# A two-stage attention kernel on one core: dummy matmuls on a tile of ones ahead of TensorE's work, and an instruction order laid out again

## The chip, the core and the metric

The kernel runs on one core of a Trainium2 chip. The core has five engines that run side by side: PE (TensorE, matmuls), DVE (VectorE), ACT (ScalarE), POOL (GpSimd) and SP (SyncE, which here only issues DMAs). The metric is the device time of one execution in microseconds; lower is better.

## The reference

```python
scores = np.matmul(q, k.transpose(0, 1, 3, 2)) / 8          # 8 batches, 8 heads, 576 rows, 64 columns
scores = np.where((rel >= 0) & (rel < 64), scores, -1e9)    # stage 1: a window of 64 keys
attn = softmax(scores)
x = (attn @ v).transpose(0, 2, 1, 3).reshape(8, 576, 512)
logits = x @ w_gate                                         # stage 2: 4 experts, the best 2 of each row
for e in range(4):
    q, k, v = x @ wq[e], x @ wk[e], x @ wv[e]               # 512 -> 64
    a = softmax(causal(q @ k.T / 8))
    out += weight[e] * (a @ v @ wo[e])                      # 64 -> 512
```

Stage 1 is attention in a window of 64 keys for 64 pairs of batch and head; stage 2 is causal attention of four experts per batch, weighted by a gate.

## The kernel before

**Work.** Stage 1 goes by units of eight blocks of 64 queries: scores (`s`), softmax on ACT, DVE and POOL, transposes (`t`) and the product with v (`a`). Two heads lie side by side on the 128 partitions as a "pair"; 32 pairs are loaded from HBM, each as q, k and v, into rings of three buffers. So the load of v for pair p waits until the last `a` block that reads pair p-3 is done, and one for q or k until the last such `s` block is. Stage 2 goes by batch and by pair of experts, 16 of these "expert pairs": projections (`K`, `k`, `Q`, `q`, `V`, `W`), scores (`1` to `4`, `0`), softmax, transposes, product with v (`A` and `B`) and the output projection (`O`, `o`). For 14 of the 16 expert pairs the transposes are done without PE: DVE transposes 32x32 blocks into the buffer `st2` and 16 DMAs move them within SBUF into `pt2` (rows `pt<-st`, `pt2<-st2`), 8 of 32x928 and 8 of 32x640 elements. I call these 16 DMAs a **set**; there are 14 sets, in the order of the expert pairs. `A` and `B` of an expert pair read the whole of its set, and its set may overwrite `pt2` only when `A` and `B` of the pair before are done. The last two expert pairs use PE transposes (`T`, `U`).

**Order.** Nothing is scheduled by hand line by line. Every instruction is recorded by a `Plan`; the string `ORDER` gives PE's blocks letter by letter, and the other engines' instructions are put in order by a small model of the core (`Plan.order`) that plays the program with costs of its own, one due time for each instruction, and the table `EARLY` of corrections to due times. Of a DMA the model takes a transfer time and `op["land"]`, the time until its data may be read. The model only lays the order out: on the chip each engine takes its instructions in that order and waits on semaphores. SP is one queue: a DMA whose buffer is not free holds up all that stand behind it. Its DMAs also share eight completion semaphores in turn, so that a DMA waits for the landing of the one eight places ahead. Every instruction is issued through line 381 (382 after the change).

**Start.** Inputs come as one stream of loads: three pairs at first and a fourth in `st2`, then the weights, then pair 4 and on. The letter `z` is a dummy block: two matmuls of `ident` with itself that nothing reads (`warm`). Six of these lie among the first blocks.

Of the kernel before, what the change touches and what calls it, by code (L numbers as in the profile page):

```python
# [34 lines left out]
    "sszzsztstazazstKKVtssQaatQsVtastkqaatzss1tV2aaVt0s3s4WVqtVVkqQ132aV4s0tKQKtksaAa"  # L35
    "B132qta40kQtKsssAaBOO1324tqOV0VOtkKaaBAsstV132a0VQtkqaABass41tVWVOVOKOtqssa3240t"
    "OKOQkaBAatVk13240qtQQsssBaAaVtVOV13240VtOQsstOOqKqaBaAatKk13240qtkssaBAWVOVtOOQs"
    "s13240VKVtOOkaaAB1324tKQk0qssaaABtOO13s24tOO0KQktqBaAa13240VtVqVVaaABOWKOOQk1324"
    "0KOVqOQVBAVkKV13240QkqBAT1TOT23T4U0TUOTUOUTUOTAUBUooUoUoUoABOOOOO"
)  # L40
EARLY = {
# [52 lines left out]
}  # L94
HOLD = 13000.0
TAIL = 2
SHORT = 0
WARM = 6
TPE = 99
BPOS = 0.05  # L100
SJOIN = 1
PARTS = ((0, 5), (5, 9))
# [294 lines left out]
def window_attention_moe_attention(ctx: ExitStack, tc: tile.TileContext, qT, kT, vW,  # L397
# [710 lines left out]
    for t, f, args in todo:  # L1108
        f(*args)
    with tc.manual_schedule():  # L1110
        nc.issue()
# [54 lines left out]
```

## Time and profile before

| what | value |
|---|---|
| median of three timed runs | 424.93 us (424.13 to 425.73) |
| the profiled execution, device time | 423.19 us |
| its span, first to last instruction | 421.5 us (1.69 us lie outside it) |
| mean granted clock of PE | 0.996 |
| PE busy | 404.1 us of 421.5 |
| loaded from HBM, written to it | 39.85 MB, 9.44 MB |

The page of the profile gives busy times by engine; the trace behind it tells what each engine waited for, which DMA landed when, and which clock PE was granted (1.00 is 2.4 GHz, 0.50 is 1.2 GHz). A float32 matmul stands in the trace as two MATMUL records, one with rounded operands (float32r) as one.

### The profile page before, as it was taken

To read this page: it belongs to the slowest core of one execution; us is meant where nothing else is said; L and a number is where in the kernel's file an instruction comes from. 1 tells how busy PE (TensorE), PEld (TensorE's weight loads), DVE (VectorE), ACT (ScalarE), POOL (GpSimd) and SP (SyncE) were. 2 spreads that over 40 slices of the span, in tenths; PEclk is the share of its full clock that TensorE was granted. 3 is DMA by queue.
4 is the path that set the end of the run, shared out by engine and by line. 5 is a ranking of instruction groups with operands and counts; after the bars stand their busy time and mean duration, and the time that the engine had idled before them with its cause. 6 is when DMAs were issued, how large, how long until landed. Compare 5 with 4: busy or idle time off the path is not lost. (4 is left out here: it accounts for less than half of the span.)

```text
span 421.5 us, 13748 instructions
## 1 busy us (share of the span) xinstructions
PE 404.1 (96%) x5168; PEld 364.4 (86%) x5168; DVE 310.3 (74%) x997; ACT 269.6 (64%) x854; POOL 276.2 (66%) x473
## 2 busy tenths in 40 slices
PE   5799999999999999999699999999899999999995
PEld 4688989999899989899598998998889999998874
DVE  4899997879876876768677878679696756456722
ACT  3676685767685858566558566585567754727932
POOL 4778777697879687695687949567759553505310
PEclk9999999999999999999899999999999999999999
DMA  7979661467876572478776366369645623642113
GB/s 241 337 260 318 187 212 59 108 167 222 283 203 188 136 252 90 122 183 299 199 223 182 136 180 201 103 157 302 173 155 139 167 56 104 166 101 54 51 51 124
DMA packets 33361, 72.66 MB, mean 172 GB/s; under 512 B 6160, under 2 KB 10256, under 8 KB 33296
## 3 DMA queue, kind: packets, MB, share of 16 engines
q1 hardware_dynamic: 32640, 71.14, 56.6%
q8 instruction: 41, 0.67, 0.6%
q10 hardware_dynamic: 656, 0.66, 0.5%
q14 instruction: 24, 0.20, 0.1%
HBM read 39.85 MB, written 9.44 MB: 117 GB/s over the span
## 5 line engine op out<-in xcount | busy, mean ns | idle before, releaser
L381 POOL TENSOR_SCALAR_AFFINE_SELECT pt<-ft 64x512 f32<-64x512 f32 x126 | 83.6, 663 | 38.2 <-ACT ft L381 29.0
L381 POOL TENSOR_TENSOR sm<-sm,st 128x512 f32<-128x512 f32 x72 | 76.5, 1068 | 34.3 <-DVE st L381 24.2
L381 POOL TENSOR_SCALAR p<-p,r,g 128x320 f32<-128x320 f32 (+4 forms) x135 | 83.5, 633 | 11.9 <-DVE r L381 10.5
L381 PE MATMUL o<-pt,v 128*64 128x64 f32 (+2 forms) x1776 | 82.5, 250 | 6.3 <-DMA pt<-st 3.2
L381 ACT ACTIVATE p<-p,r 128x192 f32<-128x192 f32 (+4 forms) x135 | 77.9, 579 | 15.8 <-DVE r L381 15.5
L381 PEld LDWEIGHTS o<-pt,v 128*64 128x64 f32 x1776 | 69.7, 139 | 20.2 <-issue 7.4
L381 DVE STREAM_TRANSPOSE st<-p 128x128 f32<-128x128 f32 (+5 forms) x126 | 63.5, 521 | 19.0 <-POOL p L381 9.9
L381 DVE CUSTOM_DVE_ANT_0 p<-s,causal 128x320 f32<-128x320 f32 (+2 forms) x120 | 52.7, 482 | 3.7 <-PE s L381 3.3
L381 DVE TENSOR_REDUCE st<-sm 128x8 f32<-128x512 f32 x72 | 47.9, 674 | 5.6 <-ACT sm L381 5.0
L381 PE MATMUL s<-k,q 64*64 64x128 f32 (+1 forms) x1116 | 37.0, 277 | 5.3 <-DMA q<-in_qT_dram 5.0
L381 PE MATMUL s<-kt,qt 64*128 64x256 f32 (+2 forms) x480 | 41.9, 317 | 0.0
L381 PEld LDWEIGHTS s<-kt,qt 64*128 64x128 f32 x480 | 35.1, 185 | 4.4 <-issue 1.8
L381 PEld LDWEIGHTS s<-k,q 64*64 64x64 f32 x1116 | 30.9, 139 | 9.2 <-DMA k<-in_kT_dram 4.5
L381 PE MATMUL kps<-xh,wkhi 128*128 128x256 f32 (+1 forms) x128 | 38.8, 303 | 0.0
L381 PE MATMUL qps<-xh,wqhi 128*128 128x320 f32 (+1 forms) x128 | 38.6, 302 | 0.0
L381 PE MATMUL v2ps<-wvhi,xh 128*128 128x260 f32 x128 | 37.8, 296 | 0.0
L381 PE MATMUL qps<-xl,wqhi 128*128 128x320 f32 (+1 forms) x128 | 37.7, 294 | 0.0
L381 PE MATMUL qps<-xh,wqlo 128*128 128x320 f32 (+1 forms) x128 | 37.6, 294 | 0.0
L381 PE MATMUL kps<-xl,wkhi 128*128 128x256 f32 (+1 forms) x128 | 37.6, 294 | 0.0
L381 PE MATMUL kps<-xh,wklo 128*128 128x256 f32 (+1 forms) x128 | 37.6, 294 | 0.0
L381 PE MATMUL v2ps<-wvhi,xl 128*128 128x260 f32 x128 | 36.3, 284 | 0.0
L381 PE MATMUL v2ps<-wvlo,xh 128*128 128x260 f32 x128 | 36.2, 283 | 0.0
(125 smaller groups left out, 928.9 us busy)
## 6 DMA issues: line engine op xcount, KB each, us to landing
v<-in_vW_dram SPq DMA_DIRECT2D x28, 576.0 KB, 5.4
pt<-st SPq DMA_DIRECT2D x112, 116.0 KB, 2.3
pt<-st SPq DMA_DIRECT2D x112, 80.0 KB, 2.1
out_dram<-out SPq DMA_DIRECT2D x32, 256.0 KB, 2.2
q<-in_qT_dram SPq DMA_DIRECT2D x28, 288.0 KB, 4.5
k<-in_kT_dram SPq DMA_DIRECT2D x28, 288.0 KB, 4.9
v<-in_vW_dram SPq DMA_DIRECT2D x3, 320.0 KB, 8.3
out_dram<-out SPq DMA_DIRECT2D x7, 128.0 KB, 2.4
```

Of the source, the lines that this page charges most:

```text
L381: call(*args, **kw)
```

## The change

Three things are changed. A tile `ones` is set on DVE, and three dummy blocks `y`, two 128x128x128 matmuls of it each, become PE's first work. In `Plan.add`, `land` grows from 1650 to 2750 ns for moves within SBUF and from 2300 to 3000 ns for loads. `ORDER` and `EARLY` are replaced by tables found for these numbers; `FIT` gets an entry for `y` (its cost is doubled in the model).

```diff
 ORDER = (
-    "sszzsztstazazstKKVtssQaatQsVtastkqaatzss1tV2aaVt0s3s4WVqtVVkqQ132aV4s0tKQKtksaAa"
...
+    "yyyszszzsztstzaazstKVtKssaaQtVsQtastkaqtass1tV2aa30tVss4WVktQqVKV1Va324s0tQqktKa"
...
 EARLY = {
-    0: 2100, 1: -1350, 2: 3350, 4: 5800, 5: 5300, 6: -8850, 7: 8050, 8: 72150, 9: 80300, 10: 5100,
...
+    3: -850, 4: 8900, 5: -7400, 6: -4000, 7: 13950, 8: 91150, 9: 75700, 10: 11400, 11: -4300, 12: 117550,
...
-            op["land"] = 1650 if len(inner) == 2 else 2300 if outs[0].space == bass.MemoryType.SB else 500
+            op["land"] = 2750 if len(inner) == 2 else 3000 if outs[0].space == bass.MemoryType.SB else 500
...
+    ones = const.tile([128, 128], F32, name="ones")
+    nc.vector.memset(ones, 1.0)
+    for k in range(3):
+        ps = psum.tile([128, 512], F32, tag="s", bufs=8, name=f"start_{k}")
+        with nc.block("y"):
+            for i in range(2):
+                nc.tensor.matmul(ps[:, 0:128], lhsT=ones, rhs=ones, start=True, stop=True)
```

Both ORDER strings hold the same number of every letter, 385 in all, and the new one three `y` more. What follows is what stands where in the built programs.

**PE, its first rows.** Before, the first block of scores stands first (`s1_0_0` and `s1_0_1` are its two banks, k0 and q0 the first pair, k1 and q1 the second):
```order
L381 MATMUL s1_0_0_108<-k0_76,q0_75 64x64 x2
L381 MATMUL s1_0_1_109<-k0_76,q0_75 64x128 x2
L381 MATMUL s1_0_0_108<-k0_76,q0_75 64x128 x2
L381 MATMUL s1_0_1_109<-k0_76,q0_75 64x128 x2
L381 MATMUL s1_0_0_108<-k1_78,q1_77 64x64 x2
L381 MATMUL s1_0_1_109<-k1_78,q1_77 64x128 x2
L381 MATMUL s1_0_0_108<-k1_78,q1_77 64x128 x2
L381 MATMUL s1_0_1_109<-k1_78,q1_77 64x128 x2
```
After:
```order
L382 MATMUL start_0_969<-ones_968 128x128 x2
L382 MATMUL start_1_970<-ones_968 128x128 x2
L382 MATMUL start_2_971<-ones_968 128x128 x2
L382 MATMUL s1_0_0_108<-k0_76,q0_75 64x64 x2
L382 MATMUL s1_0_1_109<-k0_76,q0_75 64x128 x2
L382 MATMUL s1_0_0_108<-k0_76,q0_75 64x128 x2
L382 MATMUL s1_0_1_109<-k0_76,q0_75 64x128 x2
L382 MATMUL s1_0_0_108<-k1_78,q1_77 64x64 x2
```
The three dummy blocks now precede the first scores; one `warm` block follows these (further down, not shown).

**SP, ahead of the sixth set.** v19 to v21, q22, k22, q23 and k23 are loads of stage 1's pairs, `out_1_2` and `out_1_3` stores of results, `pt2<-st2` the moves of the set. Before:
```order
L381 DMA v19_499<-in_vW_dram 128x1152
L381 DMA out_0_dram<-out_1_3_480 128x512
L381 DMA out_0_dram<-out_1_2_482 128x512
L381 DMA q22_493<-in_qT_dram 128x576
L381 DMA k22_494<-in_kT_dram 128x576
L381 DMA q23_538<-in_qT_dram 128x576
L381 DMA k23_539<-in_kT_dram 128x576
L381 DMA v20_547<-in_vW_dram 128x1152
L381 DMA v21_549<-in_vW_dram 128x1152
L381 DMA pt2_72<-st2_71 32x640 x2
L381 DMA pt2_72<-st2_71 32x928 x3
```
After, the front of the set:
```order
L382 DMA q22_493<-in_qT_dram 128x576
L382 DMA k22_494<-in_kT_dram 128x576
L382 DMA q23_538<-in_qT_dram 128x576
L382 DMA k23_539<-in_kT_dram 128x576
L382 DMA out_0_dram<-out_1_2_482 128x512
L382 DMA v19_499<-in_vW_dram 128x1152
L382 DMA v20_547<-in_vW_dram 128x1152
L382 DMA pt2_72<-st2_71 32x640
L382 DMA pt2_72<-st2_71 32x928 x2
L382 DMA pt2_72<-st2_71 32x640
L382 DMA pt2_72<-st2_71 32x928
```
After, its end:
```order
L382 DMA pt2_72<-st2_71 32x928
L382 DMA pt2_72<-st2_71 32x640 x2
L382 DMA pt2_72<-st2_71 32x928 x2
L382 DMA pt2_72<-st2_71 32x640
L382 DMA pt2_72<-st2_71 32x928 x2
L382 DMA pt2_72<-st2_71 32x640
L382 DMA v21_549<-in_vW_dram 128x1152
L382 DMA q24_544<-in_qT_dram 128x576
```
v21, the last load ahead of the set, now stands behind it; v19, which stood at the front of the stretch, now stands with v20.

**SP, ahead of the tenth set.** Before, the loads of two pairs' q and k, two stores and v27 and v28 stand ahead of the set's first moves:
```order
L381 DMA q30_703<-in_qT_dram 128x576
L381 DMA k30_704<-in_kT_dram 128x576
L381 DMA q31_748<-in_qT_dram 128x576
L381 DMA k31_749<-in_kT_dram 128x576
L381 DMA out_0_dram<-out_3_3_690 128x512
L381 DMA out_0_dram<-out_3_2_692 128x512
L381 DMA v27_709<-in_vW_dram 128x1152
L381 DMA v28_755<-in_vW_dram 128x1152
L381 DMA pt2_72<-st2_71 32x640
L381 DMA pt2_72<-st2_71 32x928 x2
```
After, with the stores that come first:
```order
L382 DMA out_0_dram<-out_3_4_688 64x512 x2
L382 DMA q31_748<-in_qT_dram 128x576
L382 DMA k31_749<-in_kT_dram 128x576
L382 DMA out_0_dram<-out_3_3_690 128x512
L382 DMA out_0_dram<-out_3_2_692 128x512
L382 DMA v27_709<-in_vW_dram 128x1152
L382 DMA pt2_72<-st2_71 32x640
L382 DMA pt2_72<-st2_71 32x928 x2
L382 DMA pt2_72<-st2_71 32x640
L382 DMA pt2_72<-st2_71 32x928
```
q30 and k30 went ahead of the ninth set, and v28 stands behind the tenth (not shown).

**SP, ahead of the eighth set.** After, the loads that stand there:
```order
L382 DMA out_0_dram<-out_2_2_584 128x512
L382 DMA q27_643<-in_qT_dram 128x576
L382 DMA k27_644<-in_kT_dram 128x576
L382 DMA q28_649<-in_qT_dram 128x576
L382 DMA k28_650<-in_kT_dram 128x576
L382 DMA v24_600<-in_vW_dram 128x1152
L382 DMA v25_652<-in_vW_dram 128x1152
L382 DMA pt2_72<-st2_71 32x640 x2
```
Before, q28 and k28 stood ahead of the ninth set; the eighth had q27, k27, two stores, v24 and v25 ahead of it:
```order
L381 DMA q27_643<-in_qT_dram 128x576
L381 DMA k27_644<-in_kT_dram 128x576
L381 DMA out_0_dram<-out_2_3_582 128x512
L381 DMA out_0_dram<-out_2_2_584 128x512
L381 DMA v24_600<-in_vW_dram 128x1152
L381 DMA v25_652<-in_vW_dram 128x1152
L381 DMA pt2_72<-st2_71 32x928 x2
```
The eighth set got one pair's loads more in front of it.

## Rows read from the trace of the kernel before

**Rows 1.** The page: the span, and busy time of each engine with its share and instructions.
```profile
span 421.5 us, 13748 instructions
PE 404.1 (96%) x5168; PEld 364.4 (86%) x5168; DVE 310.3 (74%) x997; ACT 269.6 (64%) x854; POOL 276.2 (66%) x473
```

**Rows 2.** Waits of PE over the whole span: us in total, times, longest.
```profile
PE s L381 <- DMA q<-in_qT_dram: 5.0, 3, 4.5
PE o L381 <- DMA pt<-st: 3.2, 1, 3.2
PE t L381 <- DVE r L381: 0.6, 1, 0.6
```

**Rows 3.** Timeline of PE: start, length, engine, line, operation, [idle before, who ended it].
```profile
207.70 6.13 PE L381 MATMUL o<-pt,v 128*64 128x256 f32 x108 [3.17 <-DMA pt<-st]
...
304.04 2.97 PE L381 MATMUL o<-pt,v 128*64 128x256 f32 x44 [1.30 <-issue]
...
324.31 4.83 PE L381 MATMUL o<-pt,v 128*64 128x256 f32 x108
```

**Rows 4.** Two stretches: busy of PE, PEld, DVE, ACT, POOL; granted clock; DMA share; GB/s.
```profile
205.00:207.70 2.70, 0.00 (x1) 0.03 (x1) 0.58 (x2) 0.38 (x2) 0.00 (x0) 0.86 0.70 142
207.70:210.00 2.30, 2.30 (x12) 1.52 (x14) 2.27 (x7) 0.63 (x1) 1.92 (x3) 0.50 0.96 359
```

**Rows 5.** Timeline of SP: DMA issues of the fourth set, and ahead of and in the sixth.
```profile
137.15 11.42 SPq L381 DMA_DIRECT2D pt<-st  x16
...
189.10 0.86 SPq L381 DMA_DIRECT2D v<-in_vW_dram  x2
191.34 14.64 SPq L381 DMA_DIRECT2D pt<-st  x16
```

**Rows 6.** SP's own waits from 180 to 214 us: total, times, longest.
```profile
SPq L381 <- DMA v<-in_vW_dram: 2.4, 2, 2.3
```

**Rows 7.** DMA issues from 137 to 150 us: count, size, median us from issue to landing.
```profile
pt<-st SPq DMA_DIRECT2D x8, 80.0 KB, 2.1
```

**Rows 8.** The same for 299.9 to 300 us, the tenth set's last move alone.
```profile
pt<-st SPq DMA_DIRECT2D x1, 80.0 KB, 3.9
```

**Rows 9.** DMA from 301 to 303 us: busy tenths in 40 slices, and the queue of instruction fetches.
```profile
DMA  2096889495120000000000009399989906064099
...
q8 instruction: 1, 0.02, 4.0%
```

**Rows 10.** Timeline of DVE and PE in the first 25 us, columns as in rows 3.
```profile
0.89 0.17 DVE L381 MEMSET tri<- 128x128 f32 x1 [0.89 <-PEq L1152]
...
4.51 1.13 PE L381 MATMUL s<-k,q 64*64 64x64 f32 x16 [4.51 <-DMA q<-in_qT_dram]
...
9.16 2.07 PE L381 MATMUL warm<-ident 128*128 128x128 f32 x8
...
18.11 0.71 PE L381 MATMUL warm<-ident 128*128 128x128 f32 x4
...
22.93 0.67 PE L381 MATMUL s<-k,q 64*64 64x64 f32 x16 [0.33 <-DMA k<-in_kT_dram]
...
24.03 0.36 PE L381 MATMUL kps<-xh,wkhi 128*128 128x256 f32 x1
```

**Rows 11.** Three stretches of the start, columns as in rows 4.
```profile
4.51:9.16 4.65, 4.18 (x65) 3.08 (x65) 1.96 (x5) 0.90 (x5) 1.12 (x10) 1.00 0.96 303
9.16:12.77 3.61, 3.61 (x42) 3.22 (x41) 2.32 (x6) 1.91 (x5) 2.50 (x3) 1.00 0.97 294
12.77:24.03 11.26, 8.76 (x156) 6.83 (x153) 10.73 (x19) 7.95 (x17) 7.96 (x10) 1.00 1.00 360
```

**Rows 12.** Timeline of PE: one matmul after a change of shape, two after others alike.
```profile
196.24 0.36 PE L381 MATMUL qps<-xh,wqhi 128*128 128x256 f32 x1
196.44 0.28 PE L381 MATMUL qps<-xl,wqhi 128*128 128x256 f32 x1
196.56 0.28 PE L381 MATMUL qps<-xh,wqlo 128*128 128x256 f32 x1
```

More of the change, by code (lines that the diff above doesn't have):

```diff
@@ L34 @@
 ORDER = (
-    "sszzsztstazazstKKVtssQaatQsVtastkqaatzss1tV2aaVt0s3s4WVqtVVkqQ132aV4s0tKQKtksaAa"
[L36 to L39, printed above, removed]
+    "yyyszszzsztstzaazstKVtKssaaQtVsQtastkaqtass1tV2aa30tVss4WVktQqVKV1Va324s0tQqktKa"
+    "AsaB132a0tkQq4sstKsAaBOqO13240OtVkVOtVVssaABatK132aatQ0qkssBaA14tVOWOKOOtVss324t"
+    "0VqQVkOqaBaA1324atK0QktKsssaAaBQOtO13240OktOVQtVsssAaaBKVqtq1324t0VkaaBAWOqQsstK"
+    "VOs13240OkVOVVtOaBA1324at0QqKsstkaABaK13tOOs240OqQtkOaABa3124q0VtVVVaaBAWOOKOkQK"
+    "13240QkKOOqBA13240VVVVQkq1ABTOTOT3T4U2U0TUOUTOUTATBUoUoUoUoUoABOOOOO"
 )
 EARLY = {
[52 rows of a table removed]
[53 rows of a table added]
 }
@@ L114 @@
     FIT = {"s": 0.979, "a": 1.008, "A": 1.008, "B": 1.012, "t": 0.975, "T": 0.975, "U": 0.975, "V": 1.024, "W": 1.024,
-           "K": 1.014, "Q": 1.014, "k": 1.013, "q": 1.013, "O": 1.015, "o": 1.015, "1": 0.966, "2": 0.984, "3": 0.969,
+           "y": 2.0, "K": 1.014, "Q": 1.014, "k": 1.013, "q": 1.013, "O": 1.015, "o": 1.015, "1": 0.966, "2": 0.984, "3": 0.969,
            "4": 0.945}
```

103 rows, old and new, of the table EARLY are left out of this document.

## The prediction

> **What bounds the kernel now.** I read the page first. PE is busy for 404.1 of 421.5 us [rows 1]; no other engine is near it, so time is won only where PE stands idle or runs slowly. The idle time is 17.4 us. The list of PE's waits and its timeline say where. 4.51 us pass before the first scores, whose q has not landed [rows 2, 10]. Another 0.47 us lie before 9.16 us and 2.50 us between 12.77 and 24.03 us, as the busy times of three stretches show (4.65 - 4.18 and 11.26 - 8.76) [rows 11]. From the first projection at 24.03 us [rows 10] on, PE hardly ever waits: 3.17 us ahead of the block at 207.70 us, 1.30 us ahead of the one at 304.04 us [rows 3], 0.56 us for a softmax [rows 2]. What remains is mostly the tail after the last matmul, which the change leaves alone.
>
> The two long waits are those of `A`/`B` blocks for their set of 16 moves, the sixth set and the tenth. The first also cost clock: PE was granted 0.86 in the 2.7 us of the wait and 0.50, the lower level of 1.2 GHz, in the 2.3 us after it [rows 4]. So the same 108 matmuls took 6.13 us there and 4.83 us at 324.31 us [rows 3]: 1.30 us more. The two late sets together cost 3.17 + 1.30 + 1.30 = 5.77 us.
>
> Why were they late? In the sixth set SP issued the loads of v20 and v21 at 189.10 us, and the 16 moves took 14.64 us to issue, where an undisturbed set took 11.42 [rows 5]. In this stretch SP itself stood for 2.3 us in one piece until a load of v had landed [rows 6]: the eighth move takes over the semaphore of v21, and its place in the queue is eight behind it. In the tenth set it was the last move: 3.9 us from issue to landing [rows 8] against 2.1 [rows 7], 1.8 us late. From 301 to 303 us the DMA engines stand nearly still for twelve slices of 0.05 us, and one fetch of instructions falls into this stretch [rows 9]. That the fetch made the hole is not shown.
>
> **The change, part by part.**
>
> *Late sets.* The new numbers act only through the order. Ahead of the sixth set stood q22, k22, q23, k23, v20 and v21; now v19 has joined them and v21, the last to be released and to land, stands behind the set. So no move waits for v21's semaphore; the 2.3 us of SP go, and of the 3.17 us of PE 0.87 are left. Against these stand 1.1 us (2750 - 1650 ns) more that the order allows for a landing. I take 0.3 us left: -2.87 us. Bounds: nothing gained if v19 and v20 land as late as v21 did (0), all of it gained (-3.17). With a wait of 0.3 us the clock stays up, as it did at 304.04 us, where 44 matmuls after a wait of 1.30 us took 2.97 us [rows 3]: -1.30, bounds 0 and -1.30. Ahead of the tenth set v28, q30 and k30 are gone from the queue, and 1.1 us more are allowed: 0.2 of the 1.30 us left, -1.10; bounds 0 and -1.30. I keep the 0.2 because a fetch beside the last move can come again, as it did there [rows 9]. The Trainium skill (Runtime: NRT & Kernel Launch, "Instruction fetch mechanics") says that crossing a block of instructions is mostly hidden; by that the hole would have another cause, the 0.2 would go too, and the sum would be 0.2 lower.
>
> *Dummies.* DVE sets `tri` from 0.89 to 1.06 us [rows 10] and `ones`, as large, right after it, so PE can begin at about 1.3 us. Three blocks are 12 records; eight `warm` records took 2.07 us at 9.16 us [rows 10], so 12 take 3.1 us and end at 4.4 us, before the first scores can start at 4.51. They cost nothing; if q and k came 0.5 us sooner they would cost that.
>
> What do they bring? At 9.16 us a record cost 0.26 us, at 18.11 us 0.71 / 4 = 0.18 [rows 10]. So the array ran at the lower level up to about 12.8 us, although the stretches there show 1.00 [rows 11]; I take the durations. PE was busy for 4.18 + 3.61 = 7.79 us in that time [rows 11]; at full clock it would be 3.9. But PE is not what sets 24.03 us. The DMA engines are at 0.96, 0.97 and 1.00 of their time in the three stretches [rows 11]: the inputs are one saturated stream, and the scores at 22.93 us waited for pair 4's k, which came out of it 0.33 us after all else was ready [rows 10]. After 12.77 us PE already runs at full clock with 2.50 us to spare. Loads of the same bytes stand ahead of that k after the change. A faster PE finds only more idle time: I take -0.2 us, bounds 0 and -0.33 (the wait before the k block). The first pair's k now stands second in ACT's queue; its scores may start up to half a microsecond later, hidden by the same stream; so is the `warm` block that now follows them (four records, 1.0 us at the lower level).
>
> *PE's own work.* The same blocks, so the same matmuls. The number of places where the shape changes from one block to the next goes from 186 to 190 after the first projection, counted in the strings by operand rows and type. A change costs 0.20 us from start to start where the next matmul costs 0.12 [rows 12], 0.08 more. Four are 0.3 us: +0.3, bounds 0 and +0.7.
>
> *New waits.* All engines' orders are new, and I can't see from the order what will be late. The eighth set got q28 and k28 in front of it, 0.58 MB more. Its late moves would cost like the tenth set's. Twelve sets waited for nothing before. I take +0.7 us, bounds 0 and 4.5 (one more wait of 3.17 us with its clock).
>
> Sum: 423.19 - 2.87 - 1.30 - 1.10 - 0.2 + 0.3 + 0.7 = 418.7 us for an execution like the profiled one. The three timed runs lie 0.94 to 2.54 us above the profiled execution; their median is 1.74 above it. If that is late landings, which vary, part of it goes too; I add 0.5 us: **419.2 us**.
>
> **Rivals.**
>
> *The early clock shortens the start.* The Trainium skill (TensorE: Matmul & The Clock Gate, Part 1) says that the array starts at half clock and that sustained work lifts it; the 0.26 and 0.18 us agree. If the chain through the first softmax, not the loads, sets 24.03 us, most of the 3.9 us come back, say 3.3: 415.9 us. That PE idles for 2.50 us behind a late start [rows 11] would allow it; the DMA share of 1.00 there and the wait for k speak against it.
>
> *The sixth set stays late.* v19 (0.58 MB) has moved right ahead of it, and with v20 and two pairs' q and k 2.3 MB still land just before. If a v load holds a semaphore as before, 2.87 and 1.30 us are not won: 419.2 + 4.2 = 423.4 us, no difference that can be told. Against it: v20 is released by an earlier `a` block than v21 was.
>
> *Slower.* Loads taken away from two sets lie in front of others: the eighth (q28, k28) and the eleventh (v28, v29 and v30 in place of v29 and v30). If both become late enough for PE to wait 3.17 us and lose 1.30 us of clock, that is 8.9 us on top, 428.1 us. It decides from waits of about 3 us on; waits like the 1.30 us one leave a gain. For it speaks that a set has no second way: SP is one queue. Against it: the twelve other sets had room, and the order now leaves 1.1 us more.
>
> **How the numbers follow.** Forecast 0.62, early clock 0.10, sixth set late 0.17, slower 0.05, something between (new waits about as long as those removed) 0.06. The range from 416.0 to 424.0 us holds the forecast, the late sixth set and half of the early clock; the forecast's own is 417 to 421.5. A measurement of this kernel tells 0.5%, 2.1 us, from no change: faster is below 422.8 us. Forecast, early clock and a little of the third case give 0.75, the rest of the third and the last 0.19, slower 0.06.
>
> **What would show it.** In the new profile: no wait of `o<-pt` for `pt<-st` above 1 us and no stretch with a clock below 1.00 after 15 us; v21 issued after the sixth set, whose issues take near 11.4 us; the dummy records from about 1.3 to 4.4 us; the `warm` records of the first 10 us at 0.18 us or less, and yet the first projection within 0.5 us of 24.03. I am wrong if the first projection starts before 23 us (early clock), if a set is still awaited for 2 us or more, or if waits on other engines add up to more than 3 us.

## The result and the profile after

The changed kernel took 420.42 us (median of four runs, 419.56 to 421.27), the kernel before, beside it, 424.69 us (424.13 to 425.73). The ratio is 0.9897, its 95% interval 0.9867 to 0.9926: faster by 1.0%. Two later series, on two chips, gave 0.9908 (0.987 to 0.9945) and 0.9917 (0.9885 to 0.995). The range of 416 to 424 us holds the time, 1.2 us above the predicted 419.2. The profiled execution took 419.56 us, against 423.19 before.

The page, as in [rows 1], its span (PE was busy for 405.8 us of it):

```profile
span 417.8 us, 13777 instructions
```

PE's waits, as in [rows 2] (us in total, times, longest), this time all of them:

```profile
PE o L382 <- POOL pt L382: 1.6, 2, 1.3
PE s L382 <- DMA k<-in_kT_dram: 1.6, 2, 1.3
PE start L382 <- DVE ones L382: 1.2, 1, 1.2
PE t L382 <- POOL sm L382: 0.9, 3, 0.3
PE o L382 <- DMA v<-in_vW_dram: 0.8, 1, 0.8
PE s L382 <- DVE yl L382: 0.6, 2, 0.4
PE o L382 <- DVE r L382: 0.6, 1, 0.6
PE kps L382 <- DVE xl L382: 0.4, 1, 0.4
```

The row `PE o <- DMA pt<-st` of [rows 2] is gone: no set is awaited. PE's timeline around the blocks that waited in [rows 3]:

```profile
205.46 4.83 PE L382 MATMUL o<-pt,v 128*64 128x64 f32 x108
...
299.00 5.13 PE L382 MATMUL o<-pt,v 128*64 128x64 f32 x108
```

Both groups begin with a block of stage 1 (32 records). `A` and `B`, the blocks that read a set, follow at 206.45 and 300.23 us; the last moves of their sets landed at 205.14 and 300.14 us. So the sixth set had 1.31 us of room and the tenth 0.09. No wait stands ahead of either, and the first group of 108 records takes 4.83 us, not 6.13. The two stretches of [rows 4], columns as there (the granted clock stands behind the five engines):

```profile
205.00:207.70 2.70, 2.70 (x82) 2.38 (x76) 2.54 (x8) 1.38 (x6) 2.65 (x5) 1.00 0.91 338
207.70:210.00 2.30, 2.30 (x50) 1.87 (x48) 2.30 (x7) 1.79 (x4) 2.30 (x4) 1.00 0.99 318
```

SP at the sixth set, as in [rows 5]:

```profile
191.33 10.95 SPq L382 DMA_DIRECT2D pt<-st  x16
```

The set starts at the same time as before (191.33 and 191.34 us), but its 16 issues take 10.95 us instead of 14.64: SP's waits show no load of v any more, so no move waits for a load's semaphore. v21 follows at 202.38 us.

The start went the other way. PE's timeline, with the row of before for the scores of pairs 2 and 3 ahead of it:

```profile
7.24 0.92 PE L381 MATMUL s<-k,q 64*64 64x64 f32 x14 [0.28 <-DMA q<-in_qT_dram]
```

```profile
1.25 2.93 PE L382 MATMUL start<-ones 128*128 128x128 f32 x12 [1.25 <-DVE ones L382]
4.44 1.13 PE L382 MATMUL s<-k,q 64*64 64x64 f32 x16 [0.26 <-DMA k<-in_kT_dram]
6.88 1.13 PE L382 MATMUL s<-k,q 64*64 64x64 f32 x16 [1.30 <-DMA k<-in_kT_dram]
7.93 1.22 PE L382 MATMUL warm<-ident 128*128 128x128 f32 x4
9.09 0.92 PE L382 MATMUL s<-k,q 64*64 64x64 f32 x14
...
11.00 1.97 PE L382 MATMUL warm<-ident 128*128 128x128 f32 x8
...
25.88 0.36 PE L382 MATMUL kps<-xh,wkhi 128*128 128x256 f32 x1
26.63 0.39 PE L382 MATMUL kps<-xl,wkhi 128*128 128x256 f32 x1 [0.39 <-DVE xl L382]
```

The dummies ran as forecast, 1.25 to 4.18 us, but the clock did not come up early: a `warm` record at 11.00 us still costs 0.25 us, about as much as at 9.16 us in [rows 10]. The second pair's k, now third in ACT's queue, was awaited for 1.30 us; then a `warm` block took 1.2 us; so the scores of pairs 2 and 3 began at 9.09 us instead of 7.24. The first projection began at 25.88 instead of 24.03. Both are 1.85 us later. What lies between is told by the chain of work that ended last in the whole execution, here its part before 26 us (start, length, what; pieces left out):

```profile
1.72 5.11 DMA k<-in_kT_dram
...
8.01 1.15 PE warm L382 x4
...
18.73 1.05 POOL sm L382
...
25.97 0.61 DVE xl L382
```

This part begins with the load of the second pair's k and takes in the `warm` block. From 11.15 us on it runs through softmaxes on DVE, POOL and ACT, and at its end through DVE's work on the weights (`wklo`, `wvlo`) and on `xl`, the second operand of the projection. No later load stands in it. Pair 4's k, awaited for 0.33 us before [rows 10], is not awaited here.

The account of the profiled execution, 423.19 - 419.56 = 3.63 us gained:

| part (us) | predicted | measured | from |
|---|---|---|---|
| the two late sets and the lost clock | -5.27 | -5.77 | [rows 3, 4] and the rows above |
| start, to the first projection | -0.2 | +1.85 | 24.03 and 25.88 us |
| shapes and new waits, first projection to last matmul | +1.0 | +0.60 | 393.12 us before, less 5.77, and 387.95 after |
| last matmul to the end of the span (what lies outside it is the same) | 0 | -0.30 | 4.32 and 4.02 us |
| from the profiled execution to the median | +0.5 | +0.86 | 420.42 - 419.56 |

### The profile page after: what moved, and what is told of

Read it like the earlier page. It is cut to its first block, busy times and chain, and to the rows that moved or that the text cites. A ratio compares the mean times of both kernels' runs of the same rounds, so it can differ in the third digit from the quotient of the medians.

```text
span 417.8 us, 13777 instructions
## 1 busy us (share of the span) xinstructions
PE 405.8 (97%) x5180; PEld 364.8 (87%) x5180; DVE 313.0 (75%) x998; ACT 268.5 (64%) x854; POOL 274.8 (66%) x473
## 4 chain that ended last, share of the span: by engine, by line
PE 82%; DVE 9%; DMA 2%; issue 2%; SPq 2%; POOL 1%; ACT 1%; ACTq 0%; DVEq 0%; POOLq 0%
PE o L382 17%; PE s L382 15%; PE kps L382 11%; PE ops L382 11%; PE qps L382 11%; PE v2ps L382 11%; PE t L382 5%; DVE st L382 3%; DVE pt L382 2%; SPq L382 2%; DVE sm L382 1%; DMA k<-in_kT_dram 1%; DVE xl L382 1%; POOL sm L382 1%; DVE g L382 1%
## 5 line engine op out<-in xcount | busy, mean ns | idle before, releaser
L382 POOL TENSOR_SCALAR p<-p,r,g 128x320 f32<-128x320 f32 (+3 forms) x135 | 83.4, 632 | 12.9 <-DVE r L382 11.3
L382 ACT ACTIVATE p<-p,r 128x320 f32<-128x320 f32 (+4 forms) x135 | 77.7, 578 | 15.2 <-DVE r L382 14.7
L382 PE MATMUL o<-pt,v 128*64 128x64 f32 (+2 forms) x1776 | 80.5, 248 | 3.0 <-POOL pt L382 1.6
L382 PEld LDWEIGHTS o<-pt,v 128*64 128x64 f32 x1776 | 68.1, 138 | 16.8 <-POOL pt L382 3.1
L382 PE MATMUL kps<-xh,wkhi 128*128 128x320 f32 (+1 forms) x128 | 38.9, 304 | 0.0
L382 PE MATMUL qps<-xh,wqhi 128*128 128x256 f32 (+1 forms) x128 | 38.9, 304 | 0.0
L382 DVE COPY_PREDICATED sm<-own,s 128x256 f32<-128x256 uint8 x72 | 29.2, 436 | 12.1 <-ACT sm L382 9.6
L382 PE MATMUL kps<-xl,wkhi 128*128 128x320 f32 (+1 forms) x128 | 37.8, 295 | 0.4 <-DVE xl L382 0.4
L382 PE MATMUL kps<-xh,wklo 128*128 128x320 f32 (+1 forms) x128 | 37.7, 294 | 0.0
L382 PE MATMUL qps<-xh,wqlo 128*128 128x256 f32 (+1 forms) x128 | 37.7, 294 | 0.0
L382 PE MATMUL qps<-xl,wqhi 128*128 128x256 f32 (+1 forms) x128 | 37.6, 294 | 0.0
```

The lines of the kernel that those rows point to most:

```text
L382: call(*args, **kw)
```

## The experiments

Besides the unedited change, each kernel is an edit of the laid-out order, made after the model has run (`done` is the list of instructions, `self.ops[n]` instruction number n), or of one number. By an edit of the list nothing else moves; by the one number other rows move a little, but no load changes its place against a set. The 12 runs were taken in three series of four, each series on one chip with the kernel before beside it.

**One load.** The kernel before with v21 moved behind the sixth set (instruction 1315 is the set's last move):

```diff
+        v21 = self.ops[1385]
+        done.remove(v21)
+        done.insert([o["n"] for o in done].index(1315) + 1, v21)
```

> The kernel before, with one instruction moved: the load of v21 stands behind the sixth set's 16 moves instead of ahead of them. Theory A (the lane of v21's semaphore held SP for 2.3 us and made the set late): the wait of 3.17 us and the clock of 0.50 are gone, the set's issues take 11.4 us instead of 14.64, the tenth set may still be late (1.3 us): median 4 us below that of the kernel before when both of its late sets are late, 420 us, and a narrower spread. Rival (v19, v20 and four loads of q and k land late anyway): a wait of 2 us or more stays, time as before.

419.91 us median (419.31 to 422.75) against 424.71 for the kernel before beside it, ratio 0.9906 (0.9872 to 0.994). PE's block, a stretch behind it and SP's set:

```profile
205.96 4.25 PE L385 MATMUL o<-pt,v 128*64 128x256 f32 x88 [1.73 <-DVE st L385]
```

```profile
205.96:208.00 2.04, 2.04 (x34) 1.78 (x36) 2.04 (x6) 0.25 (x1) 1.32 (x2) 1.00 0.88 322
```

```profile
191.22 13.14 SPq L385 DMA_DIRECT2D pt<-st  x16
```

The profile names DVE at the block, but the set's last move landed at 205.82 us: it is the set that was awaited, 1.73 us instead of 3.17. The clock stayed at 1.00, and the tenth set was awaited for 0.7 us. So theory A holds for the clock and the time; that the wait would be gone and the issues would take 11.4 us was wrong, they took 13.14. SP stood 1.8 us for a load of v still: v20, the next one ahead, landed at 198.06 us. In the profiled execution (419.82 us, 3.37 below that of the kernel before) the sixth set's wait gave 1.44 us, the clock 1.30 and the tenth set's wait 0.60. One instruction gives the whole gain of the change, within the intervals.

**The same load in the changed kernel**, put back ahead of the set:

```diff
+        v21 = self.ops[1385]
+        done.remove(v21)
+        done.insert([o["n"] for o in done].index(1302), v21)
```

> The changed kernel with the one instruction moved back: v21 ahead of the sixth set. Theory A: SP stands for v21's buffer and its semaphore again, some 2.3 us and more; of the 1.31 us of room that the sixth set had nothing is left, TensorE waits 1 to 3 us for it and may lose clock behind it: 421.5 to 424.5 us. Rival (the larger allowance and the other rows of the order are what made room): no wait above 0.5 us, 420.4.

420.95 us (419.9 to 424.5) beside 420.19 for the changed kernel; ratio to before 0.9936 (0.9905 to 0.9967), which is not told apart from the 0.9908 of the changed kernel. Theory A is wrong here by size, and the rival is nearer. SP's waits from 180 to 214 us, its timeline, and PE's blocks for the sixth and the eighth set:

```profile
SPq L386 <- PE o L386: 6.6, 5, 4.2
```

```profile
187.25 7.08 SPq L386 DMA_DIRECT2D v<-in_vW_dram  x3
194.42 10.83 SPq L386 DMA_DIRECT2D pt<-st  x16
```

```profile
206.86 2.37 PE L386 MATMUL o<-pt,v 128*64 128x256 f32 x54 [0.52 <-DMA pt<-st]
...
252.79 1.52 PE L386 MATMUL o<-pt,v 128*64 128x256 f32 x12 [1.53 <-DVE xl L386]
```

In the changed order v21's buffer comes free later. SP stands 4.2 us for it and the set starts 3.1 us later than in the changed kernel; but in that time the loads in flight land, so the moves wait next to nothing for a semaphore (v21 lands at 198.87 us, the eighth move goes out at 198.88; 10.83 us in all), and the set is awaited for 0.52 us only. The longest wait for a set lies elsewhere: the eighth set's last move landed at 252.49 us, and its block stood 1.53 us. The two unedited runs of the changed kernel in these series show 0.48 and 1.07 us there, so little of it can be laid to v21. The place of v21 cures the order before; in the changed order there is room without it.

**The tenth set.** The changed kernel with v28 put back ahead of that set (1975 is its first move):

```diff
+        v28 = self.ops[2052]
+        done.remove(v28)
+        done.insert([o["n"] for o in done].index(1975), v28)
```

> The changed kernel with one instruction moved back: the load of v28 ahead of the tenth set instead of behind it. Theory A (the loads ahead of a set decide when it lands): v28's buffer comes free some 2 us after the set could start, SP stands for it, the tenth set, which had 0.09 us of room, is awaited for 1 to 2.5 us at about 300 us: 421.5 to 422.5. Rival (only the slow landing of the last move made that wait): no wait above 0.5 us there, 420.2.

424.42 us (421.18 to 425.87) beside 420.25 for the changed kernel; ratio to before 1.0004 (0.9975 to 1.0032). The whole gain is gone. SP's timeline in the changed kernel at the set, then in this one with the loads ahead of it, and PE's block:

```profile
286.31 11.30 SPq L382 DMA_DIRECT2D pt<-st  x16
```

```profile
281.62 7.78 SPq L386 DMA_DIRECT2D v<-in_vW_dram  x2
289.49 11.63 SPq L386 DMA_DIRECT2D pt<-st  x16
```

```profile
302.79 3.90 PE L386 MATMUL o<-pt,v 128*64 128x256 f32 x76 [2.45 <-DMA pt<-st]
```

SP stood 7.0 us for v28's buffer (its row of waits for `PE o` says 11.4 us in two, the longest 7.0), the set began 3.2 us later, and PE waited 2.45 us for it. The wait is as long as theory A said; the time is 2 us above its 421.5 to 422.5. The profiled execution took 422.1 us, the second fastest of twelve, with a mean granted clock of 1.000; the other eleven had 0.986 to 0.998. That they lost clock behind the wait is likely, but where they lost it is not shown.

**The allowance alone.** The kernel before with the new numbers for `land` and its own `ORDER` and `EARLY`:

```diff
-            op["land"] = 1650 if len(inner) == 2 else 2300 if outs[0].space == bass.MemoryType.SB else 500
+            op["land"] = 2750 if len(inner) == 2 else 3000 if outs[0].space == bass.MemoryType.SB else 500
```

> The kernel before with only the allowance raised (2750 and 3000 ns in the model's landings), its own order of blocks and table of due times kept. No load changes its place against a set by that. Theory A: the gain comes from the places of v21, v28, q30 and k30, which only the new tables moved, so the time is that of the kernel before within 1 us, with the waits for the sixth and tenth sets. Rival (the allowance itself makes the room): 419 to 421.

424.43 us, ratio 1.0011 (0.998 to 1.0043): nothing. PE's block in its profile, again put down to another engine than the set, whose last move landed at 206.68 us:

```profile
206.87 5.33 PE L381 MATMUL o<-pt,v 128*64 128x256 f32 x74 [2.57 <-ACT sm L381]
```

The tenth set was awaited too, for 1.85 us. So the gain lies in the new tables, and the single moves above point to the places of a few loads in them.

**The dummies.** The changed kernel without them:

```diff
+        done = [o for o in done if o["n"] < 2761]
```

> The changed kernel with the order as it is, but the tile of ones and its three dummy blocks left out (they feed nothing). Theory A: the first projection starts 16.8 us after the scores of pairs 2 and 3 (24.03 - 7.24 before, 25.88 - 9.09 after), the softmaxes of the first units set it, and those scores are late because the second pair's k lands at 6.8 us and a dummy block stands ahead of them; the dummies are neutral: first projection at 25.9 us, device time 419.6 to 420.4. Rival B: the early matmuls themselves slow the first loads; then the second pair's k lands at 5.9 us, the first projection starts near 25.0, device time 419.0 to 419.5. Rival C: without them the clock comes up later than at 12.9 us and the first projection starts near 27.

419.89 us (419.13 to 421.05), ratio 0.9931 (0.9905 to 0.9957). PE's timeline:

```profile
6.30 1.13 PE L384 MATMUL s<-k,q 64*64 64x64 f32 x16 [0.82 <-DMA k<-in_kT_dram]
...
8.51 0.92 PE L384 MATMUL s<-k,q 64*64 64x64 f32 x14
...
25.84 0.37 PE L384 MATMUL kps<-xh,wkhi 128*128 128x256 f32 x1
```

The first projection is where it was, at 25.84 us, and the time too. The clock came up at 10.8 us, not later than in the changed kernel's profile: rival C is out. For rival B nothing speaks: the second pair's scores start at 6.30 us here, and with the dummies at 6.88, 6.13 and 6.47 us in the three profiles of the changed kernel. By theory A the first projection should have stood at 8.51 + 16.8 = 25.3 us; here the clock fell back to 0.50 from 21.1 to 24.5 us, which can account for the rest; that is argued, not shown.

**The order of the first loads.** The changed kernel with pair 0, 1, 2's k in that order:

```diff
+        for loads in ((1, 3, 5), (15, 17, 19)):
+            at = [i for i, o in enumerate(done) if o["n"] in loads]
+            for i, n in zip(at, loads):
+                done[i] = self.ops[n]
```

> The changed kernel with only the first loads of k (first part and second part) put back into the order pair 0, 1, 2. Theory A (the chain through the first softmaxes): pair 1's k lands near 5.9 us, the scores of pairs 2 and 3 start near 8.1 instead of 9.09, the first projection near 24.9 instead of 25.88; device time 1.0 us less than the changed kernel, 419.4 by medians. Rival (one saturated stream of loads sets the first projection): it stays at 25.9 and the time at 420.4, since the same bytes come in the same time.

419.89 us (418.07 to 421.72), ratio 0.9938 (0.9907 to 0.9969). PE's timeline at first, and a later stretch:

```profile
4.49 2.32 PE L387 MATMUL s<-k,q 64*64 64x64 f32 x32 [0.31 <-DMA q<-in_qT_dram]
...
7.88 0.92 PE L387 MATMUL s<-k,q 64*64 64x64 f32 x14
```

```profile
20.72:27.55 6.83, 6.55 (x73) 5.80 (x70) 5.48 (x11) 4.93 (x12) 3.31 (x4) 0.50 1.04 389
```

The wait of 1.30 us for the second pair's k is gone and the scores of pairs 2 and 3 begin 1.2 us earlier, as theory A says. But in this execution PE ran at the lower level from 20.72 to 27.55 us and the first projection came at 26.40. Whether the order of the loads alone gains time stays open.

**The old start in the changed kernel.** `START` lists the 149 instructions that stand ahead of the first projection in the order before; first without the dummies, then with them (`first`):

```diff
+        first = [o for o in done if o["n"] >= 2761]
+        done = [o for o in done if o["n"] < 2761]
+        done = first + [self.ops[n] for n in START] + [o for o in done if o["n"] not in START]
```

> The changed kernel without the dummies on ones, and with every engine's order up to the first projection as in the kernel before (149 instructions), the rest as changed. Theory A: scores of pairs 2 and 3 at 7.2 us, first projection at 24.0, the whole 1.85 us of the later start come back: 418.6 by medians (417.7 for an execution like the profiled one). Rival: the late middle of the changed kernel was laid out for its own start, waits appear behind the first projection and eat it up: 420.4.

> The same, with the tile of ones and the three dummy blocks in front. Theory A: dummies change nothing, first projection at 24.0, equal to the run without them within 0.5 us. Rival (early clock): TensorE is then busy from 1.3 us without a gap longer than 0.3 us, the clock comes up well before 12.4 us, the scores of pairs 2 and 3 and the scores after them take half the time, and the first projection starts 1 to 2 us earlier, at 22 to 23; device time 417.

419.13 us (418.26 to 419.72) without and 418.96 us (418.32 to 422.03) with the dummies; ratios 0.9917 (0.9884 to 0.9951) and 0.9912 (0.9886 to 0.9938). The two kernels above, which keep the changed start, took 419.89 in the same series, 0.8 and 0.9 us more; the unedited changed kernel was not in it. The first projection is at 24.41 and 24.39 us; a `warm` block that the splice left ahead of it takes 0.4 us of that. So 1.47 of the 1.85 us come back at the first projection, and about half of it shows in the time. PE's timeline with the dummies:

```profile
7.13 0.56 PE L393 MATMUL s<-k,q 64*64 64x64 f32 x14 [0.65 <-DMA q<-in_qT_dram]
...
8.16 1.16 PE L393 MATMUL warm<-ident 128*128 128x128 f32 x8
10.44 1.10 PE L393 MATMUL s<-k,q 64*64 64x128 f32 x32 [1.12 <-DMA q<-in_qT_dram]
...
16.79 1.30 PE L393 MATMUL o<-pt,v 128*64 128x64 f32 x32 [1.58 <-DMA v<-in_vW_dram]
...
22.87 0.67 PE L393 MATMUL s<-k,q 64*64 64x64 f32 x16 [1.11 <-DMA k<-in_kT_dram]
...
24.39 0.37 PE L393 MATMUL kps<-xh,wkhi 128*128 128x256 f32 x1
```

Here the dummies did what they can do: the `warm` records at 8.16 us take 0.145 us each, the clock is up. PE then waits 1.12 us for q, 1.58 for v and 1.11 for pair 4's k, and the first projection starts when it did without them. The rival of the early clock is out for this start: the waits for loads take all of it.

**The changed kernel again, twice**, as the base of the second and third series:

> The changed kernel once more, unedited, as the base of this call. Both theories: 420.4 us median; no wait of TensorE for a set above 0.5 us and no clock below 1.00 between 28 and 410 us. The time at which the clock comes up may differ from 12.71 us (it was 10.5 and 10.8 in two executions whose first 10 us hold the same work or less); if it comes up near 10.5, the first projection still starts within 0.5 us of 25.9.

> The changed kernel unedited, as the base of this call. Both theories: 420.2 us; first projection between 25.0 and 25.9, whenever the clock comes up.

420.19 us (418.54 to 422.38) and 420.25 us (418.41 to 421.66). No set was awaited for more than 0.5 us in either, but for the eighth in the third series: its block stood 1.07 us, and the set's last move landed 0.31 us before it went on. In the second series the clock came up at 10.0 us, the scores of pairs 2 and 3 began at 8.34 us and the first projection at 25.09, so not within 0.5 us of 25.9 as expected; the distance is 16.75 us. In the profile of the third the clock was up from the first scores, and still the first projection came at 25.77 us:

```profile
4.37 0.67 PE L382 MATMUL s<-k,q 64*64 64x64 f32 x16 [0.19 <-DMA k<-in_kT_dram]
...
19.11 2.83 PE L382 MATMUL o<-pt,v 128*64 128x64 f32 x48 [2.80 <-DMA v<-in_vW_dram]
...
25.77 0.36 PE L382 MATMUL kps<-xh,wkhi 128*128 128x256 f32 x1
```

```profile
18.04:24.86 6.82, 5.75 (x88) 5.44 (x92) 4.79 (x6) 4.93 (x9) 3.21 (x5) 0.50 1.04 402
```

PE ran ahead of the loads, waited 2.80 us for v, and was at 0.50 from 18.04 to 24.86 us. In this execution, what the early clock gave was lost again by the wait and the fall of the clock.

**Towards a faster start.** The kernel with the old start and the dummies once more, beside the changed one, and with a start edited further:

> The changed kernel with the dummies and with the old order up to the first projection, once more, beside the changed kernel on one chip. Theory A (the start of the changed order costs 1.85 us in the profile): first projection near 24.4, median 1.0 to 1.5 us below that of the changed kernel in this call. Rival (what the start gives is lost behind it, or was a matter of that chip): within 0.5 us of it.

> As old_start_again, and further: the load of wq goes behind those of pair 4's q and k, that of wo behind pair 5's, VectorE makes both xl before wvlo, and the first projection stands ahead of the third block of transposes, without the last dummy block on ident. Theory A (with the early clock the first projection waits for loads and for xl, not for TensorE): first projection at 22.6 to 23.2 us instead of 24.4, time 1.0 to 1.5 us below old_start_again. Rival (one stream of loads): it starts earlier, but the scores behind it wait for pair 5's q and k, and the time is that of old_start_again within 0.5 us.

419.71 us (418.85 to 421.84) and 420.77 us (418.55 to 423.71) beside 420.25. The old start is 0.5 us faster than the changed kernel by medians here and its ratio to before is 0.9919 (0.9889 to 0.9949) against 0.9917: not settled, and half of what theory A gave. The further edit (ratio 0.9944, 0.9917 to 0.9972) brought the first projection forward, and nothing came of it. PE's timeline:

```profile
23.51 0.38 PE L393 MATMUL kps<-xh,wkhi 128*128 128x256 f32 x1
...
40.62 0.66 PE L393 MATMUL t<-ident,sm 128*128 128x128 f32 x4 [1.12 <-POOL sm L393]
```

The code is that of the old start, with another list `START` (the loads of wq and wo, `xl` and `wvlo` as told, the first `K` ahead of the third `t`) and without instruction 45, the last dummy block:

```diff
-        done = [o for o in done if o["n"] < 2761]
+        done = [o for o in done if o["n"] < 2761 and o["n"] != 45]
```

The first projection came at 23.51 us, against 24.39 and 24.79 in the two profiles of the old start with the dummies: later than the 22.6 to 23.2 forecast. 1.12 us were lost at 40.62 us to a softmax of POOL, where the old start in the same series lost 0.45. By medians the time is 1.1 us above that of the old start, so neither theory holds. The rival, no gain, was nearer, though the place is another: not pair 5's loads.

## Why the prediction was right, and where not

*Late sets and clock: right, and a little more than predicted.* Of 5.77 us all went in the profiled execution. v21 behind the sixth set is shown as a cause in the order before: moved alone it gives the gain. It is not the only one in the changed order, where v21 put back costs 0.8 us, which is within the intervals. "v19 has joined them" was loosely put: v19 stood ahead of the set before too, four loads earlier (and a load of v has 0.59 MB, not 0.58). The eighth move waits for the load eight places ahead. That was v21, which landed at 199.03 us; in the changed order it is v20, which landed at 195.44, before the move's turn. In the kernel before with v21 moved alone it is v20 too, and that landed only at 198.06. So the stretch ahead of the set did more than take one load away; which of its other moves brought v20 in earlier was not separated.

The remainder of 0.3 us that I kept did not come, nor the 0.2 for the tenth set. There the room of 0.09 us was partly luck: the last move took 3.1 us to land, slow again, but 0.8 us less than before. The loads beside the tenth set matter as much as those beside the sixth: v28 put back costs 4.2 us.

*The allowance.* "1.1 us more are allowed" stood beside the places of the loads as a second reason. Alone it does nothing (ratio 1.0011).

*The start: the term that failed.* I had written that "PE is not what sets 24.03 us" and that the later first scores and the `warm` block behind them would be "hidden by the same stream". They were not. Both chains are nearly level. With the early clock PE waits for the loads, at 24.39 us as without it, so that part was right. But when the scores of pairs 2 and 3 move by 1.85 us, the chain of softmaxes behind them becomes the longer one, and it moves with them: 24.03 - 7.24 = 25.88 - 9.09 = 16.79 us, and 25.09 - 8.34 = 16.75 in the second series. That these softmaxes set it is read from the chain in the profile after, which holds both delays and no later load. The distance itself is no constant: the seven executions with the changed start show 16.64 to 18.52 us, 17.33 or more in the three whose clock fell back to 0.50 on the way, so the equality is no proof. That the start costs time is shown by the old start put back: 0.5 to 0.9 us by medians, less than the 1.85 of the profile. I read from a wait of 0.33 us for pair 4's k [rows 10] that the stream had the last word, and bounded the term by 0 and -0.33; a loss had no bound. The row that would have said it is the span from 7.24 to 24.03 us: any delay at its front shows at its end unless the loads are later still, and the order showed two delays there, a k behind another in ACT's queue and a `warm` block. Of the 1.85 us I had named 1.5, and called them covered. The term was off by 2.05 us, and that is more than the whole difference of 1.2 us: the terms for the sets, the new waits and the end erred by 1.2 us together the other way, so part of the closeness of the sum is luck.

*The dummies' clock: right by outcome, wrong in one of its signs.* I expected `warm` records of 0.18 us or less in the first 10 us; this execution showed 0.3 at 7.93 us and 0.25 at 11.00. In others the clock came up early (below). Two of these, v21 ahead and v28 ahead of their sets, have the start of the changed kernel; their clock was up at 5.1 and 4.1 us and stayed. There the first projection does begin sooner, at 24.61 and 24.95 us, but its second operand is not ready. PE's timeline with v21 ahead:

```profile
24.61 0.36 PE L386 MATMUL kps<-xh,wkhi 128*128 128x256 f32 x1
26.25 0.38 PE L386 MATMUL kps<-xl,wkhi 128*128 128x256 f32 x1 [1.28 <-DVE xl L386]
```

PE goes on at 26.25 and 26.57 us, against 26.63 in the profile of the change: of the 1.27 and 0.93 us won, 0.38 and 0.06 are left. So the early clock gained next to nothing, as forecast, but not by the loads alone: DVE's `xl` takes what they leave. The Trainium skill (TensorE: Matmul & The Clock Gate, Part 1) says that the number of slow matmuls at a start differs from run to run; the executions here agree: in three of the changed kernel the clock was up at 4.4, 10.0 and 12.7 us.

*Shapes and new waits.* +0.60 against +1.0. The new waits behind the first projection are small, 0.39, 0.25, 0.38, 0.21 and 0.57 us, 1.80 in all against 1.00 before. The eighth set, which I had named as the danger, was not awaited in the profiled execution (0.37 us of room). Its block stood 0.48 and 1.07 us in the two other profiles of the changed kernel, and 0.76, 0.82 and 1.53 us without the dummies, with the other order of loads and with v21 put back: a small late set that comes and goes.

*The fetch beside the last move.* That the fetch of instructions made the hole of [rows 9] was left open, and no run takes a fetch away. But the traces of all 14 runs speak for it. Of the last moves of the sets whose landing is known, 76 had an instruction packet of 16 KB in flight within 2.1 us of their issue, and 72 of these took over 2.5 us to land (median 3.2, up to 4.1). Of the 119 others one took 2.5 us, the rest at most 2.3. The tenth set's last move had such a packet beside it in 12 of the 14 executions and took 3.0 to 3.9 us, and 2.06 us in the other two. In those two the set was late all the same: PE waited 2.45 us with v28 ahead of it, and 1.85 us in the kernel before with the allowance alone. So a set's last move can cost about 1 us by chance.

## What to carry to other kernels

A queue that carries both loads and the moves that the bottleneck waits for is tuned by single places: one load ahead of a set can cost or give the whole per cent (v21 in the order before, v28 in the changed one) or next to nothing (v21 in the changed one). Look first at which load each move's semaphore or each queue place has to wait for, and at when that load's buffer comes free.

Where two chains reach the same point within a few tenths of a microsecond, an idle wait at the end of one does not say that the other has room. Bound a delay at the front of either by the full delay.

Ask of dummy work for the clock whether the engine or the loads set the end of the stretch. Here it was the loads and `xl` of DVE: PE only waited sooner, and in two executions it lost the clock again.

## What the runs showed of the hardware that was not expected

The time at which the clock comes up differs between executions of the same start. With the dummies, nine profiled executions of six kernels have it at 4.1, 4.2, 4.4, 5.1, 6.2, 10.0, 10.5, 12.6 and 12.7 us of the span; without them, five have it at 10.8, 11.0, 12.0, 12.1 and 12.4. Among these, three executions of the changed kernel have 4.4, 10.0 and 12.7, and two of the old start with the dummies 6.2 and 12.6. So the dummies seem to raise it early in about half of the executions (five of nine, against none of five without), and the profile of the change happened to be one in which they did not.

Before its first rise in an execution the windows of the profile give the clock as 1.00, while the durations are those of the lower level (1.13 us for 16 records of scores at 4.44 us, 0.67 us at 4.37 us in another execution). At a start durations are to be trusted, not that column.

The kernel before varied between 419.55 and 428.11 us over some 80 timed runs in all series, the version with one load moved between 419.31 and 422.75 over nine. The longer of these runs are also those with less clock: leaving out five runs above 426 us, the 47 with a mean granted clock of 0.994 or more have a median of 422.7 us, the 28 below it 424.3. So lost clock is part of the spread; where it was lost one profile can't show.

The last moves of the sets landed 2.05 to 2.3 us after their issue (one 2.5) where no 16 KB packet of instructions was in flight beside them, and 3.2 us after it (median) where one was. So the room of a set depends on where a fetch falls.
